# A chunk's first products wait for their own pair of heads instead of for all four pairs

## The chip, the cores and the metric

The kernel runs on one core of a Trainium2 chip. The metric is the device time of one execution in microseconds (us), lower is better; 1226.58 us is the median of 3 runs before the change.

## What is computed

Attention that keeps the 32 best scores of each row, followed by two feed-forward layers on 2304 tokens of width 512:

```python
scores = scale * np.matmul(q, k.transpose(0, 1, 3, 2))          # 4 x 8 heads, 576 x 576, head size 64
kth = np.partition(scores, -top_k, axis=-1)[..., -top_k:-top_k + 1]
scores = np.where(scores >= kth, scores, -1000000000.0)
x = softmax(scores) @ v                                          # heads side by side: 2304 x 512
g = x @ w_gate                                                   # 512 -> 1536
x = (g * sigmoid(g) * (x @ w_val)) @ w_out                       # 1536 -> 512
h = x @ w_in                                                     # 512 -> 2048
out = (h * np.cos(h)) @ w_out2                                   # 2048 -> 512
```

## The kernel before

The 2304 tokens are 18 tiles of 128, and the tiles are taken in ten chunks: chunks 0 and 1 have one tile each, chunks 2 to 9 two (`SIZES`, L33). A chunk is worked through by pairs of heads (`NP` = 4 pairs). For each tile and head, a *unit* (`unit_proc`, L570): PE makes 128x576 scores, ACT copies them (L602), DVE finds the 32 best by four MAX8 (L627) and three MATCH_REPLACE8 (L630), ACT makes the exponentials (L658, L669). PE turns them (L691), multiplies them with V (L744, L747, `av_proc`), and POOL divides by the row sums: that is `x_proc` (L764), which leaves the pair's input, transposed, as `xw` in chunks 0 and 1 (L811) and as a high and a low part `x` in the others (L824, L828). One pair of heads is one 128-row K-tile of the first layer's matmul, so the four inputs of a chunk are the four terms of each of its sums.

The first layer's products of a chunk are made per block f of 128 hidden columns (12 of them). In chunks 2 to 9 `gemm_proc` (L886) takes the gate half (g = 0) and then the value half (g = 1), each in a PSUM bank of its own (`gvt[g]`, freed when ACT has copied it), with three matmuls for each pair kk (high times high, high times low, low times high, L902). Chunks 0 and 1 use plain float32 products, two blocks per bank (`turned_gemm_proc`, L979, L992). The output products follow in `wout_proc` (L1052, L1066). The last chunk (`last`) waits in addition for `ev_psb`, a change of memory pools that needs all its inputs (`pool_b_proc`, L1148).

The order on each engine is not written out. Each `..._proc` is a generator that yields either an event to wait for or a step (engine, cost, function, due time, whether it depends on the step before). `Plan.run` (L131) plays all generators against each other with those costs: it takes the engine that can start first and on it, of the steps that are ready, the one with the earliest due time. The instructions are written into each engine's list in that order, and the chip runs each list in order; waits are by semaphores. A step whose event comes earlier in the plan can therefore stand earlier in the list, and all that is planned behind it can move too. DMAs of the plan are issued from SP's queue, in order: keys (`kx`, L489), queries (`qx`, L514), V (L541, L543), output weights of the first layer (`wo`, L379), and the chain of the second layer's weights, which loads a block into one buffer (`w_raw`, L356), converts it on ACT and POOL (L245, L246, L248) and stores it (`w2d`, L360) before the next load.

Where a product waits for its input, before:

```python
        yield ev_x[c]
        yield ev_w1[f]
```

Of the kernel before, what the change touches and what calls it, by code (L numbers as in the profile page):

```python
# [34 lines left out]
NCH = len(SIZES)  # L35
TURNED = [n == 1 for n in SIZES]
FIRST = [sum(SIZES[:c]) for c in range(NCH)]
NP = H // 2
# [126 lines left out]
def topk_attention_moe_moe(ctx: ExitStack, tc: tile.TileContext, qT, kT, vP, w1, wo1, w2, out):  # L165
    nc = tc.nc
    plan = Plan()
# [384 lines left out]
    ev_exp = [Event() for _ in range(NU)]  # L552
    ev_e = {(c, p, t): Event() for c, p, t, h in units if h == 0}
    eT, smT, ptT, XH, XL, RX = {}, {}, {}, {}, {}, {}
    ev_x = [Event(NP * len(ATT[c])) for c in range(NCH)]
    ev_av, ev_rs = {x: Event() for x in parts}, {x: Event() for x in parts}
    ev_pt = {(c, p, g): Event(ATT[c][g][1]) for c, p, g in parts}
    ev_sum = {(c, p, g): Event(2 * ATT[c][g][1]) for c, p, g in parts}
# [205 lines left out]
    def x_proc(c, p, g):  # L764
        t0, n = ATT[c][g]
        key = c, p, g
        due = due_unit(unit_of[c, p, t0 + n - 1, 1]) + 12.0
        yield ev_sum[key]
        yield r_rs.gate(part_of[key])
        st = {}  # L770

        def rinv():
            sm = smT[key]
            nc.vector.reciprocal(sm, sm)

        yield ("POOL", 0.18, lambda: nc.gpsimd.tensor_scalar(smT[key], smT[key], 1e-9, None, op0=OP.add), due,
               True)
        yield "DVE", 0.09, rinv, due, True

        def spread():  # L780
            rx = att.tile([128, 4, 64], F32, tag="rx", name="rx")[:, :2 * n]
            RX[key] = rx.rearrange("p a b -> p (a b)")
            nc.gpsimd.tensor_scalar(rx, smT.pop(key)[:, :, None].to_broadcast([128, 2 * n, 64]),
                                    1.0, 1.0, op0=OP.mult, op1=OP.mult)

        yield "POOL", 0.15 + 0.11 * n, spread, due, True
        k = tp_count[0]
        tp_count[0] += 1
        yield r_tp.gate(k)

        def turn():
            st["ps"] = psR.tile([128, 4, 128], F32, tag="tp", name="tp", bufs=r_tp.n)
            for t in range(n):
                nc.tensor.transpose(st["ps"][:, t], RX[key][:, t * 128:t * 128 + 128], ident)

        yield "PE", 0.11 * n, turn, due, True

        def fetch():
            st["x"] = att.tile([128, CH], F32, tag="rs", name="rs")[:, :n * 128]
            nc.scalar.activation(st["x"].rearrange("p (a b) -> p a b", a=n), st["ps"][:, :n], AF.Copy)  # L800

        end = yield "ACT", 0.07 + 0.1 * n, fetch, due, True
        r_tp.free(k, end, plan)
        ev_rs[key].set(end, plan)
        yield ev_av[key]
        cols = slice(t0 * 128, (t0 + n) * 128)
        if c < PLAIN:

            def whole():
                XH[c, p] = xslot[p // 2][:, p % 2, c * 128:c * 128 + 128]  # L810
                nc.gpsimd.tensor_mul(XH[c, p], RX[key], st["x"])  # L811

            end = yield "POOL", 0.05 + 0.0025 * n * 128, whole, due, True
            r_rs.free(part_of[key], end, plan)
            ev_x[c].set(end, plan)
            return
        yield "POOL", 0.05 + 0.0025 * n * 128, lambda: nc.gpsimd.tensor_mul(st["x"], RX[key], st["x"]), due, True
        yield r_x.gate(x_index(c, p))

        def hi():  # L820
            if (c, p) not in XH:
                x = xp.tile([128, 2, MH], F32R, tag="x", name="x", bufs=NX)
                XH[c, p], XL[c, p] = x[:, 0], x[:, 1]
            nc.scalar.activation(XH[c, p][:, cols], st["x"], AF.Copy)  # L824

        yield "ACT", 0.07 + 0.1 * n, hi, due, True
        end = yield ("POOL", 0.05 + 0.0026 * n * 128,
                     lambda: nc.gpsimd.tensor_sub(XL[c, p][:, cols], st["x"], XH[c, p][:, cols]), due, True)  # L828
        r_rs.free(part_of[key], end, plan)
        ev_x[c].set(end, plan)  # L830

# [52 lines left out]
    def gemm_proc(c, f):  # L886
        k = K0[c] + f
        due = moe_due(c, f)
        if f:
            yield ev_gemm[c, f - 1]  # L890
        yield ev_x[c]
        yield ev_w1[f]
        last = c == NCH - 1
        if last:
            yield ev_psb
        n = SIZES[c] * 128
        gv, done = {}, [Event(), Event()]

        def part(g, kk):
            xh, xl = XH[c, kk][:, :n], XL[c, kk][:, :n]  # L900
            for i, (a, m) in enumerate(((0, xh), (0, xl), (1, xh))):
                nc.tensor.matmul(gv[g], W1[f, kk // 2][:, a, g, kk % 2], m, start=kk == 0 and i == 0,  # L902
                                 stop=kk == KT - 1 and i == 2)

        rings = []
        for g in range(2):
            if last:
                ring, i = r_o[(2 * f + g) % NLAST], (2 * f + g) // NLAST
                yield ring.gate(i)
                gv[g] = pools["psB"].tile([128, DM], F32, tag=f"o{(2 * f + g) % NLAST}", name="gvl")[:, :n]  # L910
            else:
                ring, i = r_gv[g], GV0[c] + f
                yield ring.gate(i)
                gv[g] = gvt[g][:, :n]
            rings.append((ring, i))
            for kk in range(KT):
                end = yield "PE", 0.08 + 0.00117 * n, lambda g=g, kk=kk: part(g, kk), due, False
                if g and f == NF1 - 1:
                    r_x.free(x_index(c, kk), end, plan)
            if not last:  # L920
                plan.start((gate_proc, val_proc)[g](k, n, gv[g], ring, i, due, done[g]), end + plan.LAT["PE"])
            elif not g:
                plan.start(tanh_proc(k, n, gv[g], due, done[g]), end + plan.LAT["PE"])
        ev_gemm[c, f].set(end, plan)
        if last:
            done[1].set(end + plan.LAT["PE"], plan)
            yield done[0]
            yield done[1]
            yield r_vv.gate(k)
            th = TH.pop(k)  # L930
            if f == NF1 - 1:
                ev_tanh.set(done[0].time, plan)

            def silu():
                VV[k] = wide("vv", n)
                nc.vector.scalar_tensor_tensor(VV[k], th, 1.0, gv[0], op0=OP.add, op1=OP.mult)

            def product():
                nc.vector.scalar_tensor_tensor(VV[k], VV[k], 0.5, gv[1], op0=OP.mult, op1=OP.mult)

            end = yield "DVE", 0.36, silu, due - 80.0, True
            rings[0][0].free(rings[0][1], end, plan)
            r_th.free(k, end, plan)
            end = yield "DVE", 0.36, product, due - 80.0, True
            rings[1][0].free(rings[1][1], end, plan)
            vv = VV[k]
        else:
            for g in range(2):
                yield done[g]
            th, hg, vv = TH.pop(k) + VV.pop(k)  # L950
            mul = 0.05 + 0.0026 * n
            yield ("POOL", 0.05 + 0.00135 * n,
                   lambda: nc.gpsimd.tensor_scalar(th, th, 1.0, 0.5, op0=OP.add, op1=OP.mult), due, True)
            yield "POOL", mul, lambda: nc.gpsimd.tensor_mul(th, th, hg), due, True
            end = yield "POOL", mul, lambda: nc.gpsimd.tensor_mul(vv, th, vv), due, True
            r_th.free(k, end, plan)
        yield r_g.gate(G0[c] + f)

        def hi():
            G[c, f] = [wide(f"g{a}1", n, F32R) for a in "hl"]  # L960
            nc.scalar.activation(G[c, f][0], vv, AF.Copy)  # L961

        yield "ACT", 0.07 + 0.00092 * n, hi, due, True
        eng, name, cost = (nc.vector, "DVE", 0.33) if last else (nc.gpsimd, "POOL", 0.05 + 0.0025 * n)
        end = yield name, cost, lambda: eng.tensor_sub(G[c, f][1], vv, G[c, f][0]), due - 80.0 * last, True  # L965
        r_vv.free(k, end, plan)
        ev_g[c, f].set(end, plan)
# [11 lines left out]
    def turned_gemm_proc(c, fp):  # L979
# [2 lines left out]
        due = moe_due(c, 2 * fp)  # L982
        if fp:
            yield ev_gemm[c, 2 * fp - 1]
        yield ev_x[c]
        ring, i = r_gv[fp % 2], GV0[c] + fp // 2
        yield ring.gate(i)
        bank = gvt[fp % 2].rearrange("p (f g n) -> p f g n", f=2, g=2)
# [1 line left out]
        def part(j, kk):  # L990
            w = W1X[2 * fp + j, kk // 2]
            nc.tensor.matmul(bank[:, j], XH[c, kk], w[:, :, kk % 2], start=j == 0 and kk == 0, stop=kk == KT - 1,  # L992
                             skip_group_check=True)

        for j in range(2):
            yield ev_w1x[2 * fp + j]
            for kk in range(KT):
                end = yield "PE", 0.44, lambda j=j, kk=kk: part(j, kk), due, False
            ev_gemm[c, 2 * fp + j].set(end, plan)
        if fp == NF1 // 2 - 1:  # L1000
# [146 lines left out]

    def pool_b_proc():  # L1148
        for c in range(NCH):
            yield ev_x[c]  # L1150

        def swap():
            pools.pop("psR").release()
# [624 lines left out]
```

## Time and profile before

| what | value |
|---|---|
| median of 3 runs | 1226.58 us (1225.91 to 1227.77) |
| profiled execution | 1224.92 us, span 1222.8 us |
| PE busy | 1174.4 us, 96% of the span |
| DVE busy | 1002.2 us, 82% |
| ACT busy | 936.1 us, 77% |
| POOL busy | 575.9 us, 47% |
| mean granted clock of PE | 0.993 |

The span is the time from the first to the last instruction on the core. Busy time is the time in which an engine has an instruction running; PE's matmuls overlap, so a busy PE need not be at its peak. The granted clock is a share of full speed. An idle time is put down to the instruction that ended it.

### The profile page before, as it was taken

The page shows a single profiled execution, that of the slowest core. Times are in us where ns is not written, and L with a number is a line of the kernel's source. Part 1 is how long each engine was busy: PE and PEld are TensorE (multiplying, and loading weights), DVE is VectorE, ACT ScalarE, POOL GpSimd, SP SyncE. Part 2 cuts the span into 40 slices and gives each one's busy share as a digit, 9 for nine tenths or more (in the row PEclk, how much of TensorE's full clock was granted, in tenths as well). Part 3 has the DMA queues.
Part 4 walks back from the last instruction along what each step waited for, and adds up shares of the span by engine and source line. Part 5 has one row for each costly group of instructions (what it writes and reads, how often), then busy time and mean ns, then how long its engine had stood idle before and what let it go on. Part 6 is the DMA issues. An engine that isn't in the chain of part 4 may idle for free.

```text
span 1222.8 us, 23301 instructions
## 1 busy us (share of the span) xinstructions
PE 1174.4 (96%) x7720; PEld 1019.1 (83%) x7720; DVE 1002.2 (82%) x1984; ACT 936.1 (77%) x2085; POOL 575.9 (47%) x1036
## 2 busy tenths in 40 slices
PE   6699988999999999999999999999999999999998
PEld 3477647898888898888888898989999998888887
DVE  7999999999999999999999997177867778644441
ACT  4789999899889889898898887445866678755651
POOL 5898976777677776787767665300000000000000
PEclk9899989999999999999999999999999999999999
DMA  7555556665555665556645433464444276443430
GB/s 260 167 175 168 183 166 197 204 201 185 181 177 172 197 194 156 170 178 196 195 153 188 155 100 102 163 202 131 140 159 138 108 246 204 146 121 104 129 103 26
DMA packets 138985, 199.95 MB, mean 164 GB/s; under 512 B 19313, under 2 KB 88433, under 8 KB 138865
## 3 DMA queue, kind: packets, MB, share of 16 engines
q1 hardware_dynamic: 138704, 198.40, 51.5%
q8 instruction: 61, 1.00, 0.3%
q14 instruction: 60, 0.48, 0.1%
q10 hardware_dynamic: 160, 0.07, 0.0%
HBM read 152.28 MB, written 46.14 MB: 162 GB/s over the span
## 4 chain that ended last, share of the span: by engine, by line
PE 58%; DVE 7%; DMA 6%; ACT 5%; POOL 3%; issue 2%; SPq 0%; POOLq 0%; ACTq 0%; DVEq 0%
PE b L1678 16%; PE b L1401 13%; PE gv L902 10%; PE y L1066 7%; DVE m L627 3%; DVE w L630 3%; PE av L747 2%; PE gvl L902 2%; PE sc L597 2%; PE tp L691 2%; DMA wo<-wo 2%; DMA kx<-in_kT 1%; DMA w2d<-w_raw 1%; DMA w_raw<-in_w 1%; DMA qx<-in_qT 1%
## 5 line engine op out<-in xcount | busy, mean ns | idle before, releaser
L627 DVE MAX8 m<-w 128x8 f32<-128x576 f32 x432 | 311.1, 748 | 1.8
L902 PE MATMUL gv<-x,w 128*128 128x256 f32 x2016 | 283.9, 288 | 2.1 <-ACT hg L869 2.1
L902 PEld LDWEIGHTS gv<-x,w 128*128 128x128 f32 x2016 | 259.1, 190 | 9.2 <-ACT hg L869 3.2
L630 DVE MATCH_REPLACE8 w<-m,w 128x576 f32<-128x576 f32 x288 | 213.4, 743 | 0.0
L1678 PE MATMUL b<-w2o,gp 128*128 128x512 f32 x864 | 202.1, 396 | 0.0
L1678 PEld LDWEIGHTS b<-w2o,gp 128*128 128x128 f32 x864 | 162.1, 188 | 39.0
L1401 PE MATMUL b<-xc,w 128*128 128x288 f32 x1344 | 182.1, 297 | 0.1
L1401 PEld LDWEIGHTS b<-xc,w 128*128 128x128 f32 x1344 | 180.0, 188 | 1.0 <-ACT s L1488 0.4
L1066 PE MATMUL y<-wo,gh 128*128 128x512 f32 x400 | 148.6, 413 | 5.0 <-DMA wo<-wo 3.9
L658 ACT ACTIVATE e<-s,b 128x576 f32<-128x576 f32 x144 | 114.3, 795 | 9.1 <-POOL b L641 9.0
L627 DVE MAX8 m<-s 128x8 f32<-128x576 f32 x144 | 107.7, 748 | 14.7 <-ACT s L602 13.7
L669 ACT ACTIVATE e<-e,b 128x576 f32<-128x576 f32 x144 | 114.4, 794 | 2.8 <-POOL b L645 0.3
L602 ACT ACTIVATE s<-sc 128x576 f32<-128x576 f32 x144 | 95.6, 664 | 19.9 <-PE sc L590 15.2
L630 DVE MATCH_REPLACE8 w<-m,s 128x576 f32<-128x576 f32 x144 | 107.0, 743 | 0.0
L691 PE MATMUL tp<-ident,e 128*128 128x128 f32 x648 | 98.9, 276 | 6.3 <-ACT pt L697 3.4
L697 ACT ACTIVATE pt<-tp 128x512 f32<-128x512 f32 (+1 forms) x216 | 101.8, 502 | 4.2 <-PE tp L691 2.8
L1066 PEld LDWEIGHTS y<-wo,gh 128*128 128x128 f32 x400 | 74.7, 188 | 27.6 <-issue 5.9
L597 PE MATMUL sc<-K,q 128*128 128x288 f32 (+1 forms) x512 | 91.0, 304 | 2.2 <-ACT s L602 1.9
L691 PEld LDWEIGHTS tp<-ident,e 128*128 128x128 f32 x648 | 77.7, 141 | 16.5 <-ACT pt L697 6.4
L1066 PE MATMUL y<-wo,gl 128*128 128x512 f32 x208 | 86.2, 421 | 4.7 <-POOL wo L248 3.0
L965 POOL TENSOR_TENSOR gl<-vv,gh 128x256 fp32r<-128x256 f32 x84 | 62.0, 738 | 41.3 <-ACT gh L961 28.5
L597 PEld LDWEIGHTS sc<-K,q 128*128 128x128 f32 (+1 forms) x512 | 72.7, 182 | 7.8 <-ACT s L602 3.7
(115 smaller groups left out, 2095.2 us busy)
## 6 DMA issues: line engine op xcount, KB each, us to landing
wo<-wo SPq DMA_DIRECT2D x96, 512.0 KB, 3.6
gr<-gd SPq DMA_DIRECT2D x72, 256.0 KB, 3.2
w_raw<-in_w SPq DMA_DIRECT2D x32, 511.8 KB, 4.4
V<-in_vP SPq DMA_DIRECT2D x52, 256.0 KB, 2.9
w<-in_w SPq DMA_DIRECT2D x24, 511.5 KB, 5.6
kx<-in_kT SPq DMA_DIRECT2D x64, 144.0 KB, 3.1
wo<-wo SPq DMA_DIRECT2D x36, 256.0 KB, 2.9
gd<-h SPq DMA_DIRECT2D x32, 288.0 KB, 2.3
```

The lines of the kernel that those rows point to most:

```text
L597: nc.tensor.matmul(sc[:r1, s, :HALF], q[:, a, (t - t0) * 128:(t - t0) * 128 + r1], k[:, s * HALF:s * HALF + HALF], start=a == 0, stop=a == 1)
L602: nc.scalar.activation(st["s"], sc[:, :, :HALF], AF.Copy)
L627: nc.vector.max(out=st["m"][:, 8 * i:8 * i + 8], in_=st["w"] if i else st["s"])
L630: nc.vector.match_replace(out=st["w"], in_to_replace=st["m"][:, 8 * i:8 * i + 8], in_values=st["w"] if i else st["s"], imm_value=LOWEST)
L658: nc.scalar.activation(st["e"], st["s"], AF.Prelu, bias=st["b"][:, 1:2], scale=SCALE, alpha=STEEP)
L669: nc.scalar.activation(st["e"], st["e"], AF.Exp, bias=st["b"][:, 2:3], scale=1.0, accum_out=smT[c, p, g][:, j:j + 1])
L691: nc.tensor.transpose(st["ps"][:, j - j0], e[:, j * 128:j * 128 + 128], ident)
L697: nc.scalar.activation(pt[:, j0:j1], st["ps"][:, :j1 - j0], AF.Copy)
L902: nc.tensor.matmul(gv[g], W1[f, kk // 2][:, a, g, kk % 2], m, start=kk == 0 and i == 0, stop=kk == KT - 1 and i == 2)
L1066: nc.tensor.matmul(bank, m, w, start=f == 0 and n == 0, stop=f == NF1 - 1 and n == len(terms) - 1)
L1401: nc.tensor.matmul(ps[b], w[:, a, side, kk], x[:, e, kk], start=start and kk == 0 and m == 0, stop=kk == 1 and m == 2, skip_group_check=True)
L1678: nc.tensor.matmul(st["o"], g[:, a, cs], W2O[f][:, b], start=f == 0 and i == 0, stop=f == NF2 - 1 and i == 2)
```

## The change

The event of a chunk's input becomes four events, one per pair of heads. A block's products wait for the first pair before they open a bank, and each product waits for its own pair. The change of pools waits for all four, as before.

```diff
-    ev_x = [Event(NP * len(ATT[c])) for c in range(NCH)]
+    ev_x = [[Event(len(ATT[c])) for p in range(NP)] for c in range(NCH)]
...
-            ev_x[c].set(end, plan)
+            ev_x[c][p].set(end, plan)
...
-        yield ev_x[c]
+        yield ev_x[c][0]
         yield ev_w1[f]
...
             for kk in range(KT):
+                yield ev_x[c][kk]
                 end = yield "PE", 0.08 + 0.00117 * n, lambda g=g, kk=kk: part(g, kk), due, False
...
-        yield ev_x[c]
         ring, i = r_gv[fp % 2], GV0[c] + fp // 2
...
             for kk in range(KT):
+                yield ev_x[c][kk]
                 end = yield "PE", 0.44, lambda j=j, kk=kk: part(j, kk), due, False
...
     def pool_b_proc():
         for c in range(NCH):
-            yield ev_x[c]
+            for x in ev_x[c]:
+                yield x
```

The new plan gives other lists. From the last chunk's products on, all engines have the list of before; ahead of that many instructions move by a few places. Lines behind L917 of the code before are shifted by one or two in the new code.

PE, the end of chunk 1's first-layer products, before: `gv` are first-layer products (`w1` weights, `xw` inputs), `y` output products, `av` attention times V, `sc` scores, `tp` turns.

```order
L590 MATMUL sc_104<-kr_137,qr_987 128x288 x2
L794 MATMUL tp_1641<-ident_70,rx_1618 128x128 x2
L992 MATMUL gv1_101<-w1_11_807,xw1_115 128x256 x2
L1066 MATMUL y0_102<-wo_1602,gl1_1237 128x512
L744 MATMUL av_1683<-pt_1456,vtail1_107 128x256
L747 MATMUL av_1683<-pt_1456,V_1168 64x256 x8
L590 MATMUL sc_104<-kr_137,qr_987 128x288 x2
```

The same place with the change:

```order
L1067 MATMUL y0_102<-wo_1542,gh1_1112 128x512
L794 MATMUL tp_1636<-ident_70,rx_1603 128x128 x2
L691 MATMUL tp_1641<-ident_70,e_1445 128x128
L590 MATMUL sc_104<-kr_137,qr_989 128x288 x2
L744 MATMUL av_1652<-pt_1452,vtail1_107 128x256
L747 MATMUL av_1652<-pt_1452,V_1180 64x256 x8
L902 MATMUL gv0_100<-x_1483,w1_0_1217 128x256 x3
L1067 MATMUL y0_102<-wo_1615,gl1_1250 128x512
```

The attention-times-V of chunk 2's second pair and the scores now stand ahead of the eleventh output product of chunk 0 (`wo_1602` before, `wo_1615` now), and between them stands the first product of chunk 2, which takes its first pair's input `x_1483`.

PE, the first products of chunk 2, before (the four inputs are `x_1481`, `x_1748`, `x_1955`, `x_2148`):

```order
L691 MATMUL tp_2162<-ident_70,e_2038 128x128
L902 MATMUL gv0_100<-x_1481,w1_0_1216 128x256 x3
L902 MATMUL gv0_100<-x_1748,w1_0_1216 128x256 x3
L902 MATMUL gv0_100<-x_1955,w1_0_1241 128x256 x3
L597 MATMUL sc_104<-K_1948,q_2017 128x288 x4
L902 MATMUL gv0_100<-x_2148,w1_0_1241 128x256 x3
L902 MATMUL gv1_101<-x_1481,w1_0_1216 128x256 x3
```

The same place with the change (the last input is `x_2103`):

```order
L744 MATMUL av_2065<-pt_1937,vtail1_107 128x256
L747 MATMUL av_2065<-pt_1937,V_1705 64x256 x8
L1067 MATMUL y1_103<-wo_2052,gl1_1798 128x512
L1067 MATMUL y1_103<-wo_2060,gl1_1798 128x512
L1106 MATMUL y1_103<-ident_70,yo_2109 128x128 x2
L597 MATMUL sc_104<-K_2035,q_2101 128x288 x4
L597 MATMUL sc_104<-K_1284,q_2101 64x288 x4
L691 MATMUL tp_2136<-ident_70,e_2015 128x128 x4
L691 MATMUL tp_2145<-ident_70,e_2015 128x128 x4
L902 MATMUL gv0_100<-x_2103,w1_0_1243 128x256 x3
L902 MATMUL gv1_101<-x_1483,w1_0_1217 128x256 x3
```

Of the first gate half only the fourth pair's product is left here; the second's stands 40 rows and the third's 18 rows further up. The scores of the fifth unit of chunk 3 (`q_2101`), which stood ahead of the last pair's attention-times-V before, stand behind it.

SP's queue at two loads of keys, those issued near 562 and 569 us in the profile, before:

```order
L489 DMA kx<-in_kT 64x576 x2
L379 DMA wo<-wo 128x1024
L360 DMA w2d<-w_raw 128x512
L379 DMA wo<-wo 128x1024
L356 DMA w_raw<-in_w 128x2047
L489 DMA kx<-in_kT 64x576 x2
L379 DMA wo<-wo 128x1024
L514 DMA qx<-in_qT 64x2x256 x2
```

The same loads with the change:

```order
L360 DMA w2d<-w_raw 128x512
L379 DMA wo<-wo 128x1024 x2
L489 DMA kx<-in_kT 64x576 x2
L356 DMA w_raw<-in_w 128x2047
L379 DMA wo<-wo 128x1024 x2
L489 DMA kx<-in_kT 64x576 x2
L360 DMA w2d<-w_raw 128x512
L356 DMA w_raw<-in_w 128x2047
L514 DMA qx<-in_qT 64x2x256 x2
```

The second load of keys no longer stands right behind the weight load `w_raw`; the load of queries now stands right behind one.

## Rows read from the trace of the kernel before

**Rows 1.** The page: busy us (share of the span) and instructions

```profile
PE 1174.4 (96%) x7720; PEld 1019.1 (83%) x7720; DVE 1002.2 (82%) x1984; ACT 936.1 (77%) x2085; POOL 575.9 (47%) x1036
```

**Rows 2.** Busy time by stretch of the span, with granted clock

```profile
core 0: us, PE busy (x) PEld busy (x) DVE busy (x) ACT busy (x) POOL busy (x), PEclk, DMA share, GB/s
30.00:60.00 30.00, 20.27 (x127) 14.27 (x127) 30.00 (x65) 24.22 (x53) 25.79 (x47) 0.83 0.50 157
...
120.00:160.00 40.00, 36.47 (x172) 25.25 (x171) 38.63 (x78) 37.60 (x84) 38.32 (x51) 0.96 0.55 170
160.00:200.00 40.00, 34.49 (x177) 21.73 (x175) 37.77 (x76) 36.91 (x84) 24.83 (x40) 0.96 0.60 177
...
240.00:300.00 60.00, 59.77 (x469) 54.36 (x467) 59.27 (x124) 54.76 (x135) 44.07 (x81) 1.00 0.62 197
300.00:360.00 60.00, 58.88 (x418) 51.46 (x415) 59.93 (x126) 52.58 (x126) 44.31 (x83) 1.00 0.59 181
...
540.00:600.00 60.00, 58.39 (x459) 51.59 (x458) 55.44 (x111) 51.65 (x126) 43.55 (x76) 1.00 0.63 193
...
660.00:720.00 60.00, 60.00 (x448) 54.17 (x445) 59.31 (x123) 52.33 (x130) 41.20 (x80) 1.00 0.42 134
```

**Rows 3.** Chain of waits: start us, us, what

```profile
245.25 2.15 PE gv L902 x18
...
1020.43 198.81 PE b L1678 x852
```

**Rows 4.** Timeline of POOL at the inputs: start us, us, instruction

```profile
63.46 0.47 POOL L811 TENSOR_TENSOR xw<-rx,rs 128x128 f32<-128x128 f32 x1
...
136.86 0.72 POOL L828 TENSOR_TENSOR x<-rs,x 128x256 fp32r<-128x256 f32 x1
...
163.11 0.73 POOL L828 TENSOR_TENSOR x<-rs,x 128x256 fp32r<-128x256 f32 x1
...
198.43 0.74 POOL L828 TENSOR_TENSOR x<-rs,x 128x256 fp32r<-128x256 f32 x1 [0.36 <-ACT x L824]
```

**Rows 5.** Timeline of PE up to 168 us; in brackets idle before, and releaser

```profile
50.71 0.47 PE L794 MATMUL tp<-ident,rx 128*128 128x128 f32 x1 [3.41 <-POOL rx L783]
...
64.51 2.76 PE L992 MATMUL gv<-w,xw 128*128 128x256 f32 x12
...
154.27 2.07 PE L1066 MATMUL y<-wo,gl 128*128 128x512 f32 x2 [2.97 <-POOL wo L248]
...
167.84 2.01 PE L1066 MATMUL y<-wo,xw 128*128 128x512 f32 x2 [2.52 <-DMA wo<-wo]
```

**Rows 6.** Busy time by stretch, behind the two PE waits (columns of rows 2)

```profile
154.30:157.70 3.40, 3.40 (x8) 1.53 (x10) 3.37 (x8) 3.40 (x7) 3.40 (x6) 0.50 0.52 179
...
167.90:171.40 3.50, 3.50 (x7) 1.70 (x7) 3.35 (x9) 3.06 (x8) 2.32 (x6) 0.51 0.18 33
```

**Rows 7.** Timeline of PE at the scores of chunk 3's fifth unit

```profile
188.57 1.38 PE L597 MATMUL sc<-K,q 128*128 128x288 f32 x8 [0.42 <-ACT s L602]
...
195.03 1.12 PE L1066 MATMUL y<-wo,gl 128*128 128x512 f32 x2
```

**Rows 8.** Timeline of ACT, the copy of those scores

```profile
191.01 0.65 ACT L602 ACTIVATE s<-sc 128x576 f32<-128x576 f32 x1
```

**Rows 9.** Timeline of DVE, first reads of scores

```profile
196.64 0.75 DVE L627 MAX8 m<-s 128x8 f32<-128x576 f32 x1
...
582.26 0.76 DVE L627 MAX8 m<-s 128x8 f32<-128x576 f32 x1 [1.13 <-ACT s L602]
```

**Rows 10.** Timeline of SP's queue, issues of DMAs

```profile
564.17 0.33 SPq L360 DMA_DIRECT2D w2d<-w_raw  x1
...
568.23 0.33 SPq L356 DMA_DIRECT2D w_raw<-in_w  x1
568.73 1.11 SPq L489 DMA_DIRECT2D kx<-in_kT  x2
```

**Rows 11.** Waits of SP's queue: us in total, times, longest us

```profile
SPq L356 <- DMA w2d<-w_raw: 31.6, 14, 4.0
```

More of the change, by code (lines that the diff above doesn't have):

```diff
@@ L829, in x_proc @@
         r_rs.free(part_of[key], end, plan)
-        ev_x[c].set(end, plan)
+        ev_x[c][p].set(end, plan)
     G = {}
```

## The prediction

> **What bounds the kernel now.** I read the page's busy shares first, then the table by stretches, then the chain of waits, then the timelines of PE, POOL and SP around the first products of each chunk. The reader is to see in the first two that no single engine sets the time: PE is busy for 96% of the span and DVE for 82% [rows 1], but DVE is full from 30 us on and PE only later: in 30 to 60 us PE works 20.27 of 30 us, in 160 to 200 us 34.49 of 40, in 240 to 300 us 59.77 of 60; from there both stand above 55 of 60, and in 660 to 720 us PE works 60.00 of 60 [rows 2]. So the selection on DVE and the list of PE lean on each other until the attention ends, and behind it PE alone is left, up to a dense last piece of 198.81 us whose order the change doesn't touch [rows 3]. A gain has to be made while attention runs, and it counts if PE reaches the last chunk earlier.
>
> The products of chunk 2 are the first where the change can act in a full stretch. Its four inputs are written on POOL: the first begins at 136.86 us, the second at 163.11, the last at 198.43, for 0.74 us [rows 4]. Before, the first product stands in PE's list where all four are there by the plan, so the first input lies ready for some 60 us.
>
> **The change part by part.** It adds and removes no instruction: PE has 7720 matmuls either way. It only lets the planner put a product into the list when its own pair is there. What that moves is bounded by the banks: products of one half (gate, then value) are written in order, so at most three of the four pairs of the first gate half can go ahead, and only if the bank of that half is free.
>
> *Chunk 2 (a gain of 1.07 us).* By the orders shown, three products of three matmuls each now stand ahead: behind the second pair's attention-times-V, behind the turn of chunk 0's output, and among chunk 1's output products. Dense products cost 2.15 us for 18, so 0.119 us each [rows 3]; nine are 1.07 us. They leave the stretch behind 200 us, where PE is full, and land in 154 to 198 us, where PE has 5.5 us of idle time in 40 [rows 2]. I count the whole 1.07 us; the ends are 0 (the idle time there is then spent waiting for something else) and 1.07.
>
> *Chunks 3 to 9 (nothing).* In the two orders the first product of every chunk from the fourth on stands at the same place, because its bank comes free only with the last products of the chunk before, when all pairs are there. The last chunk waits for all pairs anyway, by its change of pools.
>
> *Chunk 0 (counted at nothing).* Its last input begins at 63.46 us [rows 4]. Four products now stand behind their own pairs, up to that time, and in PE's idle time: it waits 3.41 us at 50.71 alone. Each is two records, 12 of which take 2.76 us, so the four are 8 times 0.23, or 1.84 us, taken out of the stretch behind 63 us [rows 5]. What hides the gain is the chain of the converted output weights: at 154.27 PE waits 2.97 us for one of them from POOL [rows 5], and a PE that comes there 1.8 us earlier waits longer. Without that cover it is worth up to 1.84 us. Ends: 0 and a gain of 1.84; I take 0, the nearer row being the wait. The products also add waits: each stands right behind its pair's attention-times-V, so PE waits for a copy on ACT and the product on POOL, which takes 0.47 us [rows 4] (some 1 us in all, an estimate that gives the copy the same), with the next scores queued behind. Those scores have cover: DVE is full in this stretch while PE idles for 10 of 30 us [rows 2].
>
> *The wait for output weights (counted at nothing).* Before, the product that waits 2.97 us at 154.27 stood ahead of a pair's attention-times-V and the next scores; now both stand ahead of it, with the first early product. The clock granted in 154.3 to 157.7 is 0.50 and in 167.9 to 171.4 it is 0.51, of a full 1.00, each behind a PE wait, of 2.97 and of 2.52 us [rows 5, 6]. If filling the first wait keeps the clock full, some 3.40 times 0.5, or 1.7 us, come back. Ends: 0 and 1.7; I take 0, because a second wait, for a DMA, stays where it was.
>
> The Trainium skill, page "TensorE: Matmul & The Clock Gate", section "Loop structure matters more than you think", speaks against the change: it wants the K-tiles of one output back to back, since PE that waits between them goes to the low clock. By that rule the nine early products would run at 1.2 GHz and give back what they gain, and the sum would be 1.07 us less. Here they are placed one at a time between other work, and the low clock is already there in 154.3 to 157.7 us without them [rows 6], so I don't count it.
>
> *Scores of chunk 3 (a risk, counted at nothing).* The scores of its fifth unit now stand behind the last pair's attention-times-V and two output products. Before, they were issued at 188.57 [rows 7], copied from 191.01 for 0.65 us [rows 8] and read by DVE at 196.64 [rows 9]: 5.0 us of slack. Behind the attention-times-V, PE was at 195.03 [rows 7], 6.5 us later, so DVE would wait 1.5 us unless PE comes there that much earlier. Ends: 0 and a loss of 1.5; I take 0, since PE's lead above is of that size.
>
> *Loads of keys and queries (a gain of 1.13 us).* The chain of second-layer weights (load, convert, store, one buffer) starts earlier in the new plan, and its transfers stand elsewhere in SP's queue. Before, one load of keys stood right behind a weight load that had to wait for a store to land: store issued 564.17, load 568.23, keys 568.73 [rows 10]. DVE then waited 1.13 us at 582.26 for scores [rows 9]. Now two output-weight loads stand in between, the store lies further ahead, and the 4.06 us pass beside other work. I count the 1.13 us. Ends: 0, and 2.26 us, a second stall of that size, if the waits of SP's queue for such stores (31.6 us in 14 of them [rows 11]) shrink elsewhere too.
>
> The sum is 1.07 + 1.13 = 2.2 us. The profiled execution took 1224.92 us, span 1222.8 us and 2.1 us around it; it lies 1.66 us under the median of 1226.58. On the profiled execution the sum gives 1222.7 us, on the median **1224.4 us**, with 1223.3 to 1225.5 us as this case's own range (gains of 1.1 to 3.3 us).
>
> **The rivals.**
> *More of the early waits go.* The 1.84 us and the 1.7 us count in full beside the 2.2: a gain of 5.7 us, 1220.8 us. For it: DVE's own waits there, and POOL and ACT serve the pair earlier if attention-times-V stands ahead of the wait. Against: POOL is busy 38.32 of 40 us in 120 to 160 us [rows 2], so the weights come no earlier.
> *Nothing carries.* In 300 to 360 us DVE works 59.93 of 60 us [rows 2], so it is full, and a PE that is 1 us early gives its lead back there; the time is that of before, 1226 to 1226.6 us. This is also what happens if the early products only wait in PE's list.
> *A load takes the place of the one that was late (slower).* In the new queue the load of queries right behind that place stands behind a store and, directly behind it, a weight load that waits for the store to land: 4.06 us in the rows of before [rows 10]. It decides if the queries land later than DVE's next read: in that stretch DVE has no scores in reserve, as its 1.13 us wait shows [rows 9], so all 4.06 us would reach DVE and then PE, which gives 1230.6 us. For it: DVE works only 55.44 of 60 us in 540 to 600 us [rows 2], the thinnest place of the kernel. Against: the keys ahead of it now go earlier, which gives it room.
>
> **How the numbers follow.** No change can be told from one within 0.2% of 1226.58 us, 2.45 us: faster is under 1224.1 us, slower over 1229.0 us. My forecast lies beside that bound: chance 0.45, of which 0.25 within it and 0.20 under it. More of the early waits: 0.20, faster. Nothing carries: 0.12, same. The late load: 0.23, slower. Together faster 0.40, same 0.37, slower 0.23. The range runs from the first rival's end, 1219.5 us (its 5.7 us and most of the second low-clock stretch), to the last one's, 1231.0 us.
>
> **What would show it.** Right: nine products of chunk 2 ahead of its last input, the last product of chunk 2 about 1 us earlier against the last input of chunk 3, and DVE's wait behind 580 us gone. The chunk 0 part: a wait of PE for weights near 152 us as long as before or longer. The first rival: that wait under 1 us and full clock behind it. The last rival: DVE idle for 3 us or more between 560 and 610 us, with the load of queries behind the weight load. Wrong altogether: the last chunk's first product moved by more than 6 us either way.

## The result and the profile after

The changed kernel takes 1237.57 us, the median of 6 runs (1235.15 to 1241.15), beside 1227.65 us (1225.91 to 1230.88) for 6 runs of the kernel before. The ratio is 1.0080, 95% interval 1.0065 to 1.0096: slower by 0.8%, against a forecast of 1224.4 us. The profiled execution took 1237.32 us with a span of 1235.5 us. Lines of `gemm_proc` up to L913 are those of before; L1066 is now L1067.

The page's busy shares of the kernel after, to set beside [rows 1]:

```profile
PE 1177.0 (95%) x7720; PEld 1023.2 (83%) x7720; DVE 1004.2 (81%) x1984; ACT 936.8 (76%) x2085; POOL 574.5 (47%) x1036
```

The work is the same to 2.6 us on PE and 2.0 us on DVE; 12.7 us of span are new. Where PE idles shows in the stretches of the kernel after (columns of rows 2):

```profile
160.00:200.00 40.00, 31.63 (x148) 18.77 (x149) 36.67 (x73) 34.85 (x77) 24.00 (x35) 0.96 0.55 162
...
240.00:300.00 60.00, 58.72 (x466) 53.15 (x467) 59.09 (x121) 55.55 (x133) 46.34 (x78) 1.00 0.64 213
300.00:360.00 60.00, 57.28 (x414) 50.23 (x413) 58.46 (x124) 51.61 (x125) 41.89 (x79) 1.00 0.53 169
...
660.00:720.00 60.00, 59.71 (x438) 53.49 (x437) 59.09 (x122) 48.97 (x120) 40.07 (x81) 1.00 0.44 143
```

Against [rows 2], PE works 2.9 us less in 160 to 200 us, and 1.1 and 1.6 us less in 240 to 300 and 300 to 360 us, where it was all but full. The first of these isn't due to the list: two later runs of the same lists, r1 (those of before) and r2 (those of the change), work 32.34 and 32.36 us in 160 to 200 us. The early products of chunk 0 stand where the change puts them. Timeline of PE after, chunk 0:

```profile
30.01 0.39 PE L794 MATMUL tp<-ident,rx 128*128 128x128 f32 x1 [2.25 <-POOL rx L783]
...
35.16 0.70 PE L992 MATMUL gv<-w,xw 128*128 128x256 f32 x2 [0.97 <-POOL xw L811]
...
45.19 0.70 PE L992 MATMUL gv<-w,xw 128*128 128x256 f32 x2 [0.91 <-POOL xw L811]
...
55.54 0.70 PE L992 MATMUL gv<-w,xw 128*128 128x256 f32 x2 [0.97 <-POOL xw L811]
...
65.89 0.70 PE L992 MATMUL gv<-w,xw 128*128 128x256 f32 x2 [0.97 <-POOL xw L811]
```

Each waits some 0.95 us for its own pair, 3.8 us in four. In front of each lies a stretch at half clock, behind a wait for a turn; two of the four, by stretch (columns of rows 2):

```profile
30.10:33.50 3.40, 3.40 (x15) 2.61 (x17) 3.40 (x8) 2.00 (x5) 2.60 (x6) 0.51 0.00 0
40.40:43.80 3.40, 3.40 (x19) 2.61 (x19) 3.40 (x8) 2.33 (x6) 2.53 (x6) 0.50 0.70 260
```

DVE's first read of unit 16 (units are counted from 0, so this is the 17th and the first of chunk 2) begins at 90.13 us, before at 85.94, and at 88.12 in r1. So the first guess was chunk 0. At the other end, the last chunk's first product (`gvl`), before and then after, and the dense last piece in the chain of waits after:

```profile
780.54 2.68 PE L902 MATMUL gvl<-x,w 128*128 128x256 f32 x21
```

```profile
791.97 2.20 PE L902 MATMUL gvl<-x,w 128*128 128x256 f32 x17
```

```profile
1033.15 198.81 PE b L1680 x852
```

The last chunk begins 11.4 us later and the dense last piece is as long as it was [rows 3]: all but 1.3 of the 12.7 us are lost ahead of 780 us. In r1 the last chunk begins at 784.34 us, so 3.8 of the 11.4 us can come with the lists of before too. Most of the delay is there early. Chunk 3's first product, before and then after (285.03 and 293.40; 286.36 in r1):

```profile
285.03 1.20 PE L902 MATMUL gv<-x,w 128*128 128x256 f32 x8
```

```profile
293.40 1.31 PE L902 MATMUL gv<-x,w 128*128 128x256 f32 x9
```

In 66 to 250 us it is DVE, the busier engine there, that works less (third busy time), before and then after:

```profile
66.00:250.00 184.00, 171.45 (x1010) 130.31 (x1009) 177.84 (x364) 168.48 (x386) 150.92 (x240) 0.98 0.58 179
```

```profile
66.00:250.00 184.00, 165.66 (x972) 125.96 (x973) 171.77 (x349) 164.45 (x374) 146.43 (x234) 0.99 0.55 170
```

The same lists again give 178.73 (r1) and 172.10 us (r2).

### The profile page after: what moved, and what is told of

It is laid out like the page before. It is cut to its first block, busy times and chain, and to the rows that moved or that the text cites. A ratio compares the mean times of both kernels' runs of the same rounds, so it can differ in the third digit from the quotient of the medians.

```text
span 1235.5 us, 23280 instructions
## 1 busy us (share of the span) xinstructions
PE 1177.0 (95%) x7720; PEld 1023.2 (83%) x7720; DVE 1004.2 (81%) x1984; ACT 936.8 (76%) x2085; POOL 574.5 (47%) x1036
## 4 chain that ended last, share of the span: by engine, by line
PE 59%; DVE 11%; POOL 9%; ACT 8%; DMA 7%; issue 4%; SPq 1%; POOLq 0%; ACTq 0%; DVEq 0%
PE b L1680 16%; PE b L1403 13%; PE gv L902 10%; PE y L1067 7%; DVE m L627 5%; DVE w L630 5%; PE av L747 3%; PE sc L597 3%; PE tp L691 2%; DMA kx<-in_kT 2%; PE gvl L902 2%; PE sc L590 2%; DMA w_raw<-in_w 2%; POOL w L248 1%; DMA qx<-in_qT 1%
## 5 line engine op out<-in xcount | busy, mean ns | idle before, releaser
L1067 PE MATMUL y<-wo,gh 128*128 128x512 f32 x400 | 148.0, 412 | 7.0 <-DMA wo<-wo 5.3
L1067 PEld LDWEIGHTS y<-wo,gh 128*128 128x128 f32 x400 | 75.1, 189 | 27.2 <-DMA wo<-wo 4.0
L1067 PE MATMUL y<-wo,gl 128*128 128x512 f32 x208 | 86.1, 421 | 3.4 <-POOL wo L248 1.9
```

The costliest lines, as they stand in the source:

```text
L1067: nc.tensor.matmul(bank, m, w, start=f == 0 and n == 0, stop=f == NF1 - 1 and n == len(terms) - 1)
```

## Experiments

Three theories. **A:** chunk 0's own early products make the loss, by their waits and the half clock. **B:** chunk 2's early products and what moves around them make it. **C:** no product makes it; the list that the planner writes anew has more small waits than that of before. In the expectations of the first two runs C stands for any new list, whichever part is changed; behind them, for a list that is planned anew from chunk 0 on. Ratios are to runs of the kernel before on the same chip, taken beside them.

### Parts of the change

One helper makes the change for chosen chunks; two kernels differ in one line (in chunks 0 and 1 the changed code opens a bank without waiting for any pair; only in chunks 2 to 9 does the first pair come first):

```diff
+    EARLY = (0,)              # e2: range(2, NCH)
+    def x_ready(c, kk):
+        for p in [kk] if c in EARLY else range(NP):
+            yield ev_x[c][p]
...
-                yield ev_x[c][kk]
+                yield from x_ready(c, kk)
```

The third keeps the change whole but lets the planner count chunk 0's inputs as ready 3 us later; the fourth puts idle products on PE's list ahead of each turn in chunk 0, so that PE doesn't rest:

```diff
-            ev_x[c][p].set(end, plan)
+            ev_x[c][p].set(end + 3.0 * (c == 0), plan)
```

```diff
+            for _ in range(6 if c == 0 else 0):
+                nc.tensor.matmul(yt[0][:, :128], ident, ident, start=True, stop=True)
```

> Only chunk 0's products wait pair by pair; all other chunks wait for all four pairs, as before. Theory A (the four early products of chunk 0, each in PE's list right behind its own pair's attention-times-V and ahead of the next scores and turns, close a loop PE, ACT, POOL, PE, so that each pair takes longer and DVE waits for row sums): the loss is nearly all here, 1234 to 1240 us, and DVE's first read of the 17th unit's scores stands near 90.1 us as with the whole change (85.9 before). Theory B (the early products of chunk 2, with the scores, weight loads and query loads that they move): 1226 to 1230 us. Theory C (any new list costs about this much, whichever part is changed): about 1237 us here and in the next kernel too.

> Only chunks 2 to 9 wait pair by pair, chunks 0 and 1 for all four pairs; by the lists only chunk 2's products move. Theory A: 1225 to 1229 us, no slower than before. Theory B: 1234 to 1240 us. Theory C: about 1237 us.

> The whole change, but the plan is told that each input of chunk 0 is there 3 us later than it reckons: the four early products stay early, but stand behind the next scores and turns in PE's list instead of ahead of them. Theory A: the loop is open, DVE's first read of the 17th unit is at most 1.5 us later than before (87.4 us or earlier), and the time is 1225 to 1230 us. Theory B and C: still 1234 us or more, since as much moves as before.

> The whole change with every list as it is, but for six extra 128x128 matmuls in chunk 0 ahead of each pair's turn of the row sums, where PE waits 1.2 to 2.3 us (they write a bank that is not in use yet). They give PE work in its waits. If the low clock that each pair's scores and attention-times-V run at (0.50 in 30.1 to 33.5 us and three times again) carries the loss of theory A: granted clock near 1.0 there, about 1.4 us less per pair, DVE's first read of the 17th unit at 86 to 88 us, and a time 2 to 4 us under that of the whole change. If the loss is the waits alone: clock up or not, the 17th unit stays at 89.5 to 91 us and the time within 1.5 us of the whole change.

Measured: chunk 0 alone 1.0057 (1.0035 to 1.0080), chunks 2 to 9 alone 1.0007 (0.9986 to 1.0028), products later 1.0038 (1.0023 to 1.0053), filler 1.0083 (1.0057 to 1.0108). B falls: without chunk 0 nothing is lost. So does C as it stood there, which wanted a loss in the second run too: from chunk 2 on, that run's lists differ from those of before on every engine. The first run seems to speak for A. The third speaks against it: its four early products don't wait, but unit 16 is read at 89.23 us, where A expected 87.4 or earlier, and the ratio is 1.0038, where A expected the time of before. The filler speaks against A as well. Its stretch of chunk 0 (columns of rows 2):

```profile
30.00:66.00 36.00, 27.42 (x200) 22.44 (x201) 36.00 (x78) 29.89 (x65) 31.52 (x57) 1.00 0.66 206
```

The clock is full, DVE works 36.00 of 36 us, and unit 16 is read at 86.14 us, 4 us earlier than in the changed kernel. The waits of the early products are still there (0.97, 1.37, 1.51 and 0.97 us), but the half clock and the delay of chunk 0 are gone, and the kernel is as slow as with them: its PE works 297.41 of 310 us in 250 to 560 us, where the kernel before works 304.45. The loss is made anew further back.

### Neutral lists

If C holds, a list planned anew for no reason must cost something too. Four kernels are the code of before, every chunk whole, with one figure of the planner moved:

```diff
-                end = yield "PE", 0.44, lambda j=j, kk=kk: part(j, kk), due, False
+                end = yield "PE", 0.43, lambda j=j, kk=kk: part(j, kk), due, False   # n2: 0.46
...
-            ev_x[c].set(end, plan)
+            ev_x[c].set(end + 1.0, plan)                                             # n3, chunks 0 and 1
...
-            end = yield "POOL", 0.05 + 0.0025 * n * 128, whole, due, True
+            end = yield "POOL", 0.15 + 0.0025 * n * 128, whole, due, True            # n4
```

> A neutral list: the code of before, and every chunk's products wait for all four pairs as before; only the planner's figure for one product of chunks 0 and 1 is 0.43 in place of 0.44. Nothing is done earlier on purpose, but from chunk 0's products on the plan, and so all lists, come out anew. Theory A (the loss is made by chunk 0's own early products): the time of before, ratio within 0.998 to 1.002, PE idle before the last chunk's products about 45 us as before, first read of unit 104 within 3 us of before. Theory C (any list that is planned anew from chunk 0 on costs about this much, because the list of before is a good draw): ratio 1.003 to 1.009, PE idle 50 to 55 us, in many waits of some 1 us between 110 and 560 us, unit 104 read 7 to 13 us later.

> The second neutral list: the planner's figure for one product of chunks 0 and 1 is 0.46 in place of 0.44, the code of before otherwise. A: ratio 0.998 to 1.002, as the other neutral lists. C: 1.003 to 1.009, and not the same as the first neutral list, since a draw is a draw: a spread of some 0.003 among the four.

> The third neutral list: the planner counts each of the inputs of chunks 0 and 1 as ready 1.0 us later than in the code of before, so the products, still whole chunk by chunk, are planned a little later. A: ratio 0.998 to 1.002. C: 1.003 to 1.009.

> The fourth neutral list: the planner's figure for the division on POOL of chunks 0 and 1 is 0.1 us larger, the code of before otherwise. A: ratio 0.998 to 1.002. C: 1.003 to 1.009.

Measured: 1.0035 (1.0018 to 1.0052), 1.0026 (1.0007 to 1.0045), 1.0009 (0.9990 to 1.0029), 1.0056 (1.0036 to 1.0075). A expected no loss in any of the four; three lie above its 1.002, of them n2 with an interval that reaches below it. C's bound of 1.003 was too high for two, and n3 can't be told from the kernel before. A list drawn anew costs 0.3% on the mean and between 0.1 and 0.6%, with no product moved on purpose.

### The move without the plan, and the plan without the move

Two kernels part what the runs so far left tied. In x1 the plan is that of before, and the four early products of chunk 0 are issued by a process that takes no time in the plan; in x2 the plan is that of the change, and the four are held until the last pair's place. Only PE's list differs from that of before (x1) or of the change (x2).

```diff
+    def early_proc():
+        yield ev_w1x[0]
+        for kk in range(NP):
+            yield ev_early[kk]
...
+            yield "-", 0.0, early, 0.0, True
```

```diff
+                    for k2 in range(KT) if held and kk == KT - 1 else () if held else [kk]:
+                        part(j, k2)
```

x3 is before with the filler above, x4 is x1 with it.

> The list of before on every engine, with one difference: the first product of each pair in chunk 0 (four instructions) stands on PE's list right behind the place where its own pair's input is written, as in the changed kernel. Nothing is planned anew. Theory A (chunk 0's own early products make the loss): ratio 1.003 to 1.006, PE waits near 1 us in front of those products, half clock behind them, first read of unit 16 some 2 to 4 us later than before. Theory C (the lists planned anew make it): the time of before, 0.998 to 1.002, even if unit 16 is read later.

> The lists of the changed kernel on every engine, with one difference: the four early products of chunk 0 stand on PE's list together behind the last pair's input again. The plan is that of the changed kernel. A: most of the loss is gone, ratio below 1.003. C: it stays, ratio 1.005 to 1.009, whatever becomes of unit 16.

> The lists of before with six idle products ahead of each turn of row sums in chunk 0, so that PE keeps its full clock there; no plan is new. If time gained in chunk 0 reaches the end, ratio 0.997 to 0.999 (a microsecond or two from the half-clock stretch between 45 and 55 us). If it does not, as the filler on the changed kernel says, 0.999 to 1.001.

> The first run of this call (early products of chunk 0 on the list of before) with the filler of the third. A: between the two, the waits for the inputs stay and the half clock goes: 1.001 to 1.004. C: 0.998 to 1.002.

Measured: x1 1.0018 (1.0001 to 1.0035), x2 1.0073 (1.0052 to 1.0095), x3 1.0020 (1.0003 to 1.0037), x4 1.0025 (1.0010 to 1.0039). The waits came in x1 as in the changed kernel, if not one by one (0.97, 2.00, 0.91 and 0.28 us); three of them in its timeline of PE:

```profile
34.61 1.22 PE L990 MATMUL gv<-w,xw 128*128 128x256 f32 x2 [0.97 <-POOL xw L811]
...
47.33 0.70 PE L990 MATMUL gv<-w,xw 128*128 128x256 f32 x2 [2.00 <-POOL xw L811]
...
58.38 0.70 PE L990 MATMUL gv<-w,xw 128*128 128x256 f32 x2 [0.91 <-POOL xw L811]
```

They cost next to nothing at the end; taking them away from the new plan gives next to nothing back. The filler on before (x3) was expected to gain or to do nothing, and x4 lies at A's place rather than at C's; both are slower by a hair. They don't tell what a full clock is worth there: in 28 to 66 us x3 has a mean granted clock of 0.91, between the 0.87 and 0.96 of two runs of the lists of before without filler.

### The same lists again, and two more draws of the change

r1 makes the change in chunk 1 alone (`EARLY = (1,)`), which moves no instruction: a control. r2 has the lists of the change. r3 and r4 are the changed kernel with the planner's 0.44 at 0.43 and 0.46.

> The change in chunk 1 alone, which moves no instruction: all five lists are those of before. All theories: ratio 0.999 to 1.001. The profile shows another execution of the same lists; if PE's idle time before the last chunk's products comes out 3 to 6 us above the 43.4 us of the profile of before, that much of every comparison with that one profile is the execution, not the list.

> The lists of the changed kernel, timed again: ratio 1.0065 to 1.0096 if the first figure holds on this chip.

> The changed kernel with the planner's figure for one product of chunks 0 and 1 at 0.43 in place of 0.44: the change is all there, the lists are planned anew from chunk 0's end on. C (the loss is a matter of which list is drawn): some ratio between 1.001 and 1.008, with no tie to that of the changed kernel. A (the change's own early products make it): 1.006 to 1.009, as the changed kernel.

> As the run ahead of it with 0.46. C: between 1.001 and 1.008, and the two differ from the changed kernel by more than their intervals in at least one case. A: 1.006 to 1.009.

Measured: r1 1.0008 (0.9990 to 1.0026), r2 1.0082 (1.0058 to 1.0106), r3 1.0040 (1.0024 to 1.0056), r4 1.0109 (1.0089 to 1.0128). With x1 and x2 this makes a table of two by two:

| | chunk 0's four products whole | early |
|---|---|---|
| lists of before | 1.0008 (r1) | 1.0018 (x1) |
| lists of the change | 1.0073 (x2) | 1.0082 (r2) |

Down a column the ratio rises by 0.0065 and 0.0064; along a row by 0.0010 and 0.0009, inside the intervals. Neighbours in the table are from two chips, the corners that lie across from each other from one: there the lists of the change cost 0.0074 (r1 to r2) and 0.0055 (x1 to x2). **The new lists make the loss, wherever the four products stand.** (Chunk 2's nine early products are in both lists of the change; e2 has them for 1.0007, and e1 loses 1.0057 without them.) And the list of the change isn't special: the same change drawn with 0.43 costs half as much, with 0.46 a third more.

The profile of r1 came out as its expectation allowed for: PE idles 48.0 us ahead of the last chunk's products, 43.0 in the first profile of before, 52.0 after. So 5 of the 9 us between the first two profiles' idle times are no more than one execution differs from another, and the ratios carry the argument.

What goes with the loss is PE's idle time in 66 to 560 us, 494 us less PE's busy time there:

| lists | PE busy | idle | ratio |
|---|---|---|---|
| before, its first profile | 475.90 | 18.1 | |
| before again (r1) | 473.87 | 20.1 | 1.0008 |
| chunks 2 to 9 alone (e2) | 473.10 | 20.9 | 1.0007 |
| neutral, input +1 (n3) | 472.56 | 21.4 | 1.0009 |
| before with filler, products moved (x4) | 471.89 | 22.1 | 1.0025 |
| before, products moved (x1) | 471.24 | 22.8 | 1.0018 |
| neutral, 0.43 (n1) | 470.74 | 23.3 | 1.0035 |
| before with filler (x3) | 470.46 | 23.5 | 1.0020 |
| change, 0.43 (r3) | 470.31 | 23.7 | 1.0040 |
| neutral, division +0.1 (n4) | 470.07 | 23.9 | 1.0056 |
| change, put back (x2) | 468.91 | 25.1 | 1.0073 |
| chunk 0 alone (e1) | 467.79 | 26.2 | 1.0057 |
| change, products later (e3) | 467.42 | 26.6 | 1.0038 |
| neutral, 0.46 (n2) | 467.01 | 27.0 | 1.0026 |
| change | 466.10 | 27.9 | 1.0080 |
| change with filler (e4) | 464.54 | 29.5 | 1.0083 |
| change again (r2) | 463.79 | 30.2 | 1.0082 |
| change, 0.46 (r4) | 463.65 | 30.4 | 1.0109 |

Idle time and ratio rise together, loosely, with e3 and n2 idle for longer than their ratios would have it (a profile is one execution, the ratio many, and the profiles aren't all from one chip). The waits in 250 to 560 us, the longest rows of DVE and PE; columns: who waited for whom, us in total, times, longest. Before:

```profile
DVE m L627 <- ACT s L602: 2.8, 4, 1.4
DVE sm L774 <- POOL sm L776: 1.8, 3, 0.8
PE y L1105 <- ACT yo L1099: 1.4, 2, 0.7
PE y L1066 <- DMA wo<-wo: 1.3, 3, 0.6
PE tp L691 <- ACT pt L697: 1.3, 4, 0.7
```

Before again (r1, lines 6 to 9 higher):

```profile
DVE sm L780 <- POOL sm L782: 3.3, 4, 1.0
DVE m L633 <- ACT s L608: 1.4, 4, 0.6
PE y L1114 <- ACT yo L1108: 1.1, 3, 0.4
PE tp L697 <- ACT pt L703: 1.0, 3, 0.7
```

After:

```profile
DVE sm L774 <- POOL sm L776: 4.8, 4, 1.5
DVE m L627 <- ACT s L602: 3.1, 4, 1.5
PE y L1067 <- DMA wo<-wo: 2.4, 2, 1.5
PE tp L691 <- ACT pt L697: 1.7, 4, 0.8
PE gv L902 <- ACT hg L869: 1.1, 2, 0.8
PE y L1067 <- ACT pt L697: 1.0, 1, 1.0
```

The change again (r2, numbered as r1; its profile, 1246.50 us, is the slowest of its six runs):

```profile
DVE m L633 <- ACT s L608: 7.7, 5, 3.8
DVE sm L780 <- POOL sm L782: 6.6, 7, 1.7
PE y L1075 <- DMA wo<-wo: 6.0, 3, 3.4
PE tp L697 <- ACT pt L703: 2.9, 5, 0.7
```

No single wait carries it. DVE's reciprocals stand too early for their row sums, PE's products ahead of their weights or of ACT's copies: each a place at which one list waits for another. The places come with the list, and for the reciprocals the lengths too: the first to wait behind 150 us waits 0.94 us in the change, in r2 and in x2; the one near 208 us, in before and in r1, 0.41 in both. The change, then x2:

```profile
151.61 0.18 DVE L774 RECIPROCAL sm<-sm 128x4 f32<-128x4 f32 x1 [0.94 <-POOL sm L776]
```

```profile
150.03 0.18 DVE L774 RECIPROCAL sm<-sm 128x4 f32<-128x4 f32 x1 [0.94 <-POOL sm L776]
```

Before, then r1:

```profile
207.98 0.18 DVE L774 RECIPROCAL sm<-sm 128x4 f32<-128x4 f32 x1 [0.41 <-POOL sm L776]
```

```profile
209.75 0.18 DVE L780 RECIPROCAL sm<-sm 128x4 f32<-128x4 f32 x1 [0.41 <-POOL sm L782]
```

Waits for scores or for loads come back at the same places with other lengths: the longest of DVE's for scores in 250 to 560 us is 1.5 us after and 3.8 in r2.

**What stays open.** Three draws with the change (r2, r3, r4: 1.0082, 1.0040, 1.0109) have a mean of 1.0077, and 1.0067 with e3, which is a fourth; the four neutral ones have 1.0032. They overlap and are few, so whether this change's lists are worse than neutral ones on the whole isn't settled. Nor is why none of the fifteen other lists is faster than that of before (two, e2 and n3, can't be told from it). That its planner's figures were fitted with that list would explain it, and is only argued. Which of the small waits would have to go wasn't tried. No version measured here beats the kernel before.

## Why the prediction was wrong, step by step

**The bounds (right).** "A gain has to be made while attention runs, and it counts if PE reaches the last chunk earlier" held with the sign turned: PE reached it 11.4 us later (7.6 against r1), which by the prediction's own list was "wrong altogether".

**The rest of the new lists, left out of the sum (the step that failed).** The part on chunks 3 to 9 looked at the first product of each chunk, found it at the same place, which it is in both traces, and put those chunks at nothing. The other parts priced the products that move and a few neighbours. No term stood for all the rest, in which DVE's reciprocals, ACT's copies, POOL's conversions and the loads stand elsewhere from chunk 0 on. That is what costs: with the four products put back, the new lists still lose 0.0065 more than r1, some 8 us, where the sum had a gain of 2.2. It costs on the whole way, not in chunks 3 to 9 alone. Chunk 3's first product is 8.4 us late already (8.0 in r2, 1.3 in r1), and DVE works 6 to 7 us less in 66 to 250 us; in 250 to 560 us PE then idles 5.6 us before (310 less 304.45) and 5.2 in r1 (304.78), but 9.6 after (300.44) and 13.8 in r2 (296.17).

**The rivals.** "Slower" had a chance of 0.23, but for one place and 4.06 us. The load of queries does stand behind a weight load that waits for a store to land, 3.80 us after the change (store issued at 584.89, load at 588.69), yet ACT converts the queries at 594.22 without a wait for them. DVE idles 4.3 us between 560 and 610 us, against 3.7 before and 6.0 in r1, so the sign that was named, 3 us or more, was there without the change. That this rival had the direction right is luck; the loss is in many places. Of the first rival, the clock behind the early wait is full, but no gain follows.

**Chunk 2, a gain of 1.07 us (places right, gain not seen).** Products of three records stand early, at 158.74, 171.39 and 190.65. PE after, around them:

```profile
158.74 0.63 PE L902 MATMUL gv<-x,w 128*128 128x256 f32 x3
160.66 1.13 PE L1067 MATMUL y<-wo,gl 128*128 128x512 f32 x2 [1.29 <-POOL wo L248]
...
165.98 0.33 PE L691 MATMUL tp<-ident,e 128*128 128x128 f32 x1 [2.34 <-ACT pt L697]
...
171.39 0.60 PE L902 MATMUL gv<-x,w 128*128 128x256 f32 x3
173.93 0.44 PE L1106 MATMUL y<-ident,yo 128*128 128x128 f32 x2 [1.94 <-ACT yo L1100]
...
190.65 0.60 PE L902 MATMUL gv<-x,w 128*128 128x256 f32 x3
```

With chunk 2 and those behind it alone (e2) the ratio is 1.0007: a gain of 0.09% can't be told there. The rows fit the stated end of 0, idle time "spent waiting for something else".

**Chunk 0, "counted at nothing" (right for the four products, not for what they set off).** The waits came at the size given (0.91 to 0.97 us each, "some 1 us"), and they cost little: x1 adds them to the list of before for 0.0010 against r1, inside the intervals. But e1, with the new lists that these four set off and no other early product, loses 0.0057.

**The wait for output weights.** It was to stay "as long as before or longer". It shrank from 2.97 [rows 5] to 1.29 us, and two others took its place, 2.34 and 1.94 us above. These come with the lists: r1 has 2.97 again, r2 1.31, 2.35 and 1.71 us.

**The clock.** After the change PE has four stretches of 0.50 to 0.51 in chunk 0 (1.2 GHz of 2.4), each behind a wait of 1.16 to 2.25 us; before, it has one, of some 10 us. The Trainium skill, page "TensorE: Matmul & The Clock Gate", section "Loop structure matters more than you think", has PE go to the low clock when it waits long between matmuls. The rows agree only in part: in r2 three such waits are followed by the low clock, in e1 one, and in r1 the wait of 2.97 us is there while the clock stays at 1.00, where the prediction's 0.50 in 154.3 to 157.7 us [rows 6] stood behind the same wait. So the 1.7 us that were to come back weren't a matter of the order alone. What the clock is worth at the end is shown by e4: full clock, unit 16 read 4 us earlier, and a ratio of 1.0083. The prediction was right that the clock doesn't change the sum, and weighed it for chunk 2 alone, where the granted clock at the three early places is 1.00.

**Keys, a gain of 1.13 us (wrong sign).** DVE's wait for the scores of unit 110, 1.13 us before [rows 9] and 0.95 in r1, was to go. After (2.83 in r2):

```profile
595.70 0.76 DVE L627 MAX8 m<-s 128x8 f32<-128x576 f32 x1 [2.29 <-ACT s L602]
```

ACT ahead of it:

```profile
592.56 0.80 ACT L245 ACTIVATE c<-w_raw 128x512 f16<-128x512 bf16 x1 [0.47 <-DMA w_raw<-in_w]
593.48 0.66 ACT L246 ACTIVATE w_raw<-w_raw 128x512 uint32<-128x512 uint32 x1
594.22 0.42 ACT L523 ACTIVATE q<-qx 128x256 fp32r<-128x256 f32 x1
595.02 0.64 ACT L602 ACTIVATE s<-sc 128x576 f32<-128x576 f32 x1
```

The second load of keys is issued 7.5 us behind the first (575.79 and 583.28), before 6.8, so it isn't earlier, and ACT waits 0.83 us for it, before 0.79. Nor do the rows bear out that keys held those scores before: POOL ended its half of them at 577.05, and PE began the scores at 580.25, straight from other products. After, POOL's half and the scores:

```profile
588.27 1.42 POOL L500 TENSOR_TENSOR K<-kx,K 64x576 fp32r<-64x576 f32 x1 [1.35 <-ACT K L496]
```

```profile
592.16 1.22 PE L597 MATMUL sc<-K,q 128*128 128x288 f32 x8
```

What is new is ACT's list: a weight block that waits for its load, and a query, now stand ahead of the copy of the scores, which begins 1.6 us behind PE's last product for them. Before, it began right behind (581.48 and 581.51).

**Scores of chunk 3 (counted at nothing, ends 0 and 1.5 us).** The risk named didn't come: DVE reads the fifth unit's scores at 205.51 without a wait. It waits for those of other units, which had no term, 0.42 us at 215.12, 0.25 at 227.37 and 1.23 at 240.72 (1.05, 1.48 and 0.44 in r2), where before and in r1 it waits for none between 200 and 250 us.

## What to carry to other kernels

Where a planner writes the lists, a change of one event is priced as two things: the instructions that it moves on purpose, and a new draw of everything else. Make the first on the old lists, as x1 does, and take neutral draws for the second, before either is explained: here the move was worth 0.1% and the draw 0.1 to 0.6% on code that changed nothing. And a loss that can be seen early in a trace need not be the one that reaches the end; mend it alone and see whether the end follows.

## What was not expected of the hardware

One list on one chip doesn't repeat to the microsecond: 31 runs of the kernel before beside the neutral lists go from 1227.5 to 1235.9 us. Its profile, 1224.92 us, was taken another time and lies below all of them; whether the chip or the execution makes that, these runs don't tell. The half clock is part of what varies: with the same lists, chunk 0 (28 to 66 us) had a mean granted clock of 0.87 in the first profile and 0.96 in r1, whose whole span had 0.999 and was still 6.7 us longer (1229.5 against 1222.8). Two single profiles that differ by some microseconds are thus no evidence; ratios over several runs are, and so are waits that come back at the same place.
